# Preparing the sums of w_out for the half-block products earlier, splitting g on two engines, and four output buffers

## The chip, the cores and the metric

One core of one Trainium2 chip runs the whole program. The metric is the device time of one launch in microseconds, the median of three runs of the kernel before: 937.75 us (937.01 to 939.1). Engines are named as in the profile: PE (TensorE), DVE (VectorE), ACT (ScalarE), POOL (GpSimd) and SP (SyncE, which here issues every DMA).

## The reference, cut to what matters

Attention over 4 batches of 8 heads, 576 positions and 64 dimensions per head, with a causal mask and a decay taken from f, and behind it two feed-forward layers:

```python
x = attention(q, k, v, f)                 # 2304 tokens x 512
h = x @ w_in                              # 512 -> 2048
x = relu(h) ** 2 @ w_out                  # 2048 -> 512
h = x @ w_in2
g = where(h >= 1, h, where(h <= -1, 0, (h + 1) ** 2 / 4))
out = g @ w_out2
```

q, k, v and f are float32, the weights float64; the result is float32.

## The kernel before

**Precision.** Each float32 operand of a large product is held as a high and a low half (type fp32r), and each product is three matmuls: high by high, low by high, high by low. So every activation is split before PE uses it: one copy (the high half) and one subtraction (the low half). Weights arrive as 64-bit words, are decoded and split once during the first block, and are kept in DRAM in split form (scr0 to scr31, one for each of 16 chunks of 128 hidden units in each of two layers); all later blocks read them from there.

**Tiling.** The 2304 tokens are cut into four blocks of 512, 512, 512 and 768. The first three go through 96 steps: block, layer (mo), chunk fc of 128 hidden units. A step does 12 matmuls for h (h_group), the activation and split on ACT, DVE and POOL (act_group), and 12 matmuls that add to four output accumulators in PSUM (out_group). The attention of the next block runs between these steps: its products on PE, its softmax on DVE and ACT, and a transposition of the probabilities by DMA (PT<-PP). When a block's second layer is done, finish copies the accumulators to "o" buffers on ACT or DVE and stores them.

**The last block** (function last_block) has two halves of 384 tokens. Hidden chunks are taken in eight pairs, and each pair is a 2 by 2 block product done with seven products instead of eight (a Strassen scheme). That needs sums of the four quarters A11, A12, A21, A22 of the pair's w_out, S1 = A21 + A22, S2 = S1 - A11, S3 = A11 - A21, S4 = A12 - S2, and sums of the four quarters of g (held in G, sums t1 to t4). For each layer there are three phases. In phase A, pair by pair: h for four quarters, the activation into G, the sums of g, and three products (key a with A11, key c with S1, key b with S2). In phase B come the products with S4 and S3, in phase C those with the other quarters. The keys a, b and c are three pairs of accumulators; between the phases their contents are added up on DVE (p, u, w).

In phase A of the kernel before each pair loads its w_out chunks (wo<-scr), adds high and low half to full precision (wf), forms S1 to S4 (sf), splits them (sum), uses S1 and S2 at once and stores S3 and S4 to DRAM for phase B. All this is 10 vector operations, which the planner may put on DVE, POOL and in part ACT.

**Order.** Nothing is ordered by hand. Each operation is given to a planner (class Schedule) with a due time, its dependencies, its buffers and a cost for each engine that may run it. The planner walks through time, gives each engine the operation with the earliest due time among those that can start, repeats this with due times corrected from behind for several sets of weights, keeps the best, and emits the instructions in that order; each engine, and SP's DMA queue, runs its instructions strictly in order. A ring is a set of buffers of one shape, reused in turn; an operation that needs a buffer waits until the old user of it is done. Some rings: big (6, weights), wf (2), low (1), ghl (2), gh (3), gl (2), o (2), acc (4 PSUM banks).

Lines of the kernel before which the rows name: L1080 h and L1131 to L1133 output products of the first three blocks, L1282 h and L1226 to L1228 products of the last block, L1306 activation of the second layer in the last block, L1188 and L1190 additions on DVE and POOL, L608, L611, L613 copies on ACT, DVE and POOL, L620 and L622 subtractions on DVE and POOL, L904 the attention's product with v.

Of the kernel before, what the change touches and what calls it, by code (L numbers as in the profile page):

```python
# [8 lines left out]
F32 = mybir.dt.float32  # L9
# [345 lines left out]
def dve_t(n):  # L355
    return n / 960.0 + 0.07
# [27 lines left out]
NPAIR = NFC // 2  # L384


@with_exitstack
def tile_attention_moe_moe(ctx: ExitStack, tc: tile.TileContext, qkv, f, w2, outT):
# [56 lines left out]
    ring("sum", 2, [P, 4, 2, 256], F32R, late=True)  # L445
    ring("ghl", 2, [P, 2, HALF], F32R, late=True)
# [9 lines left out]
    ring("o", 2, [P, 512], F32)  # L456
# [714 lines left out]

    scr2 = [dram.tile([P, 2, 2, 256], F32, name=f"sum{i}") for i in range(2 * NPAIR)]

    def last_block():
# [7 lines left out]

        def load(due, src, dst, size, deps, bufs):
            return sch.op(due, {"SP": (dma_t(size), lambda: nc.sync.dma_start(out=dst(), in_=src()))}, deps, bufs)

        def add(due, out, a, b, width, deps, bufs, sub=False, psum=False):
            op = ALU.subtract if sub else ALU.add
            alts = {"DVE": (dve_t(width), lambda: v.tensor_tensor(out(), a(), b(), op=op), *([] if psum else [True]))}  # L1188
            if not psum:
                alts["POOL"] = (pool2_t(width), lambda: nc.gpsimd.tensor_tensor(out(), a(), b(), op=op))  # L1190
            return sch.op(due, alts, deps, bufs)

        for mo in range(2):
# [9 lines left out]
            def split(nm, due, gb, slot, deps):  # L1203

                if nm[0] in "5c" or nm[:2] == "aC":
                    ghl = new("ghl", f"ghl{nm}")
                    hi, lo = (lambda i=i: ghl.tile[:, i, :] for i in range(2))
                    bufs = [ghl]
                else:
                    gh, gl = bufs = new("gh", f"gh{nm}"), new("gl", f"gl{nm}")  # L1210
                    hi, lo = (lambda b=b: b.tile[:, :n] for b in bufs)
                src = lambda: gb.tile[:, slot, :]
                o1 = sch.op(due, copies(hi, src, n), deps, [gb, bufs[0]])
                o2 = sch.op(due + 0.5, subs(lo, src, lambda: hi().bitcast(F32), n), [o1], [gb, *bufs])
                return hi, lo, bufs, o2
# [19 lines left out]
            sums, s_store = [], []  # L1235
            pend = None
            for c in range(NPAIR):
                tA = T0 + c * t_a
                nm = f"{mo}_{c}"
                W0, W1 = new("big", f"wi{nm}"), new("big", f"wo{nm}")  # L1240
                o_w0, o_w1 = [], []
# [4 lines left out]
                for j in range(2):  # L1246
# [245 lines left out]
```

## Time and profile before

| | |
|---|---|
| three timed runs | 937.75 us median, 937.01 to 939.1 |
| the profiled execution | 942.0 us, of which the span of instructions is 940.2 us |
| PE busy | 922.1 us, 98% of the span |
| DVE, ACT, POOL busy | 705.3, 661.7, 239.0 us |
| DMA | 246.35 MB, its main queue busy 79.4% of 16 engines' span |
| granted PE clock | 1.0 of full speed throughout |

The stages in the span: attention of the first block alone up to about 45 us, the first block to about 225 us, second and third block from there to about 685 us, and the last block from about 680 us to the end, with its second layer from about 805 us. PE's idle time is 18 us in all, so the table of stretches and the list of waits are read for where these 18 us lie.

### The profile page before, as it was taken

How to read it: one execution, taken by the hardware profiler on the slowest of the kernel's cores; microseconds unless marked ns; L12 is line 12 of the kernel's file. 1: busy time of each engine (PE TensorE's matmuls, PEld its weight loads, DVE VectorE, ACT ScalarE, POOL GpSimd, SP SyncE). 2: the span in 40 equal slices, each digit the busy share in tenths (PEclk: the TensorE clock that was granted, in tenths of full speed). 3: DMA queues.
4: the chain of work that ended last, by engine and by line, in shares of the span. 5: the costliest groups of instructions: out<-in, count | busy, mean ns of one | idle time of the engine just before them, and what ended most of it. 6: DMA issues, size and time to landing. Idle time of an engine off the chain costs nothing.

```text
span 940.2 us, 14542 instructions
## 1 busy us (share of the span) xinstructions
PE 922.1 (98%) x4674; PEld 795.8 (85%) x4674; DVE 705.3 (75%) x1539; ACT 661.7 (70%) x1308; POOL 239.0 (25%) x392
## 2 busy tenths in 40 slices
PE   7999999999999999999999999999989999999998
PEld 6677778877888888888888888888889999999998
DVE  8899999899867668767777668866576656887653
ACT  7988889998878768877776777776455554455542
POOL 4300101324221322341223224242100013222234
PEclk9999999999999999999999999999999999999999
DMA  7799998997999897887789887896696656766561
GB/s 219 230 373 365 331 397 306 372 347 263 336 304 285 251 252 253 281 254 210 263 236 310 243 266 216 245 284 192 187 307 239 245 206 230 263 221 226 204 202 68
DMA packets 131868, 246.35 MB, mean 262 GB/s; under 512 B 90448, under 2 KB 91632, under 8 KB 117008
## 3 DMA queue, kind: packets, MB, share of 16 engines
q1 hardware_dynamic: 131792, 245.43, 79.4%
q8 instruction: 37, 0.61, 0.3%
q14 instruction: 39, 0.32, 0.1%
HBM read 177.57 MB, written 46.84 MB: 239 GB/s over the span
## 4 chain that ended last, share of the span: by engine, by line
PE 82%; DVE 7%; DMA 6%; ACT 3%; issue 1%; POOL 0%; ACTq 0%; DVEq 0%; POOLq 0%
PE h L1080 24%; PE h L1282 11%; PE acc L1131 8%; PE acc L1133 8%; PE acc L1132 8%; PE av L904 4%; DMA PT<-PP 2%; DMA out_dram<-o 2%; DMA wo<-scr 2%; PE s L825 2%; PE s L826 2%; PE b L1226 2%; PE b L1228 2%; PE b L1227 2%; PE a L1228 1%
## 5 line engine op out<-in xcount | busy, mean ns | idle before, releaser
L1080 PE MATMUL h<-x,whl 128*128 128x512 f32 x1128 | 291.3, 397 | 0.3 <-DVE whl L1057 0.3
L1080 PEld LDWEIGHTS h<-x,whl 128*128 128x128 f32 x1128 | 204.5, 188 | 41.6 <-issue 3.0
L1131 PE MATMUL acc<-gh,whl 128*128 128x512 f32 x384 | 152.9, 398 | 0.9 <-ACT o L608 0.9
L1133 PE MATMUL acc<-gl,whl 128*128 128x512 f32 x384 | 150.8, 393 | 0.0
L1132 PE MATMUL acc<-gh,whl 128*128 128x512 f32 x384 | 150.4, 392 | 0.0
L1133 PEld LDWEIGHTS acc<-gl,whl 128*128 128x128 f32 x384 | 72.1, 188 | 15.8
L1131 PEld LDWEIGHTS acc<-gh,whl 128*128 128x128 f32 x384 | 72.1, 188 | 14.2 <-ACT o L608 1.6
L879 DVE SCALAR_TENSOR_TENSOR PP<-E,st,PP 128x512 f16<-128x512 f32 (+2 forms) x128 | 76.6, 632 | 9.6 <-ACT PP L875 8.3
L627 DVE CUSTOM_DVE_ANT_0 E<-s,mask 128x288 f32<-128x288 f32 (+2 forms) x128 | 61.9, 500 | 28.5 <-PE s L826 16.6
L1132 PEld LDWEIGHTS acc<-gh,whl 128*128 128x128 f32 x384 | 72.2, 188 | 11.1
L842 ACT ACTIVATE E<-E,st 64x320 f32<-64x320 f32 (+2 forms) x96 | 63.6, 663 | 25.2 <-DVE st L627 15.1
L620 DVE TENSOR_TENSOR gl<-g,gh 128x512 fp32r<-128x512 f32 x76 | 55.7, 732 | 26.7 <-PE acc L1133 13.4
L1282 PE MATMUL h<-x_last,wi 128*128 128x384 f32 x384 | 72.5, 337 | 2.1 <-DVE G L1306 2.0
L1282 PE MATMUL h<-x,wi 128*128 128x384 f32 x384 | 72.5, 334 | 0.0
L875 ACT ACTIVATE PP<-E,st 128x512 f16<-128x512 f32 (+2 forms) x128 | 68.4, 591 | 5.7 <-DVE st L849 4.5
L1282 PEld LDWEIGHTS h<-x_last,wi 128*128 128x128 f32 x384 | 66.7, 188 | 4.5 <-DVE G L1306 4.4
L1282 PEld LDWEIGHTS h<-x,wi 128*128 128x128 f32 x384 | 67.1, 188 | 0.3
L613 POOL TENSOR_SCALAR pr<-PT 128x640 fp32r<-128x640 f16 (+2 forms) x55 | 32.2, 586 | 131.5 <-PE av L904 69.9
L904 PEld LDWEIGHTS av<-pr,vt 128*128 128x128 f32 x288 | 53.3, 188 | 12.9 <-ACT pr L608 1.5
L904 PE MATMUL av<-pr,vt 128*128 128x320 f32 (+2 forms) x288 | 62.1, 287 | 1.6 <-ACT pr L608 1.1
L622 POOL TENSOR_TENSOR gl<-g,gh 128x512 fp32r<-128x512 f32 x20 | 30.6, 1528 | 111.7 <-PE acc L1133 29.1
L608 ACT ACTIVATE pr<-PT 128x640 fp32r<-128x640 f16 (+2 forms) x60 | 36.1, 610 | 16.6 <-DMA PT<-PP 10.0
(352 smaller groups left out, 1904.3 us busy)
## 6 DMA issues: line engine op xcount, KB each, us to landing
whl<-scr SPq DMA_DIRECT2D x56, 1024.0 KB
raw<-in_w_dram SPq DMA_DIRECT2D x28, 1024.0 KB
scr<-whl SPq DMA_DIRECT2D x28, 1024.0 KB
wo<-scr SPq DMA_DIRECT2D x48, 512.0 KB
in<-in_qkv_dram SPq DMA_DIRECT2D x32, 608.0 KB
wi<-scr SPq DMA_DIRECT2D x32, 512.0 KB
whl<-scr SPq DMA_DIRECT2D x16, 512.0 KB
sum<-sum SPq DMA_DIRECT2D x16, 512.0 KB
```

What stands on the lines that cost most here:

```text
L608: alts["ACT"] = (act_t(n, psum), lambda: nc.scalar.activation(out(), in_(), AF.Copy))
L620: alts["DVE"] = (dve_t(n), lambda: nc.vector.tensor_sub(out(), a(), b()), True)
L627: return nc.vector.tensor_tensor_reduce(out=out, in0=ps, in1=mask[:m, OFF - q0:OFF - q0 + n], scale=scale, scalar=3e38, op0=ALU.add, op1=A ...
L842: nc.scalar.activation(Ec.tile[:m, :e], Ec.tile[:m, :e], AF.Exp, scale=-1.0, bias=nmx(), accum_out=st.tile[:m, 1, ci:ci + 1])))}, [*tops, ...
L875: nc.scalar.activation(hi, x, AF.Copy, scale=r())
L879: nc.vector.scalar_tensor_tensor(lo, x, r(), hi, op0=ALU.mult, op1=ALU.subtract)
L904: nc.tensor.matmul(av.tile[:, c0:W], vt.tile[:, kc, :, :], pr.tile[:, i, :n], start=(kc == 0 and i == 0), stop=(kc == NK - 1))
L1080: nc.tensor.matmul(ps.tile[:, :n], w.tile[:, 0, wi, kc * P:(kc + 1) * P], src.tile[:, kc, xi, :n], start=(kc == 0 and i == 0), stop=(kc == ...
L1131: nc.tensor.matmul(a.tile[:, :n], wh, gh.tile[:, :n], start=(fc == 0), stop=False)
L1132: nc.tensor.matmul(a.tile[:, :n], wl, gh.tile[:, :n], start=False, stop=False)
L1133: nc.tensor.matmul(a.tile[:, :n], wh, gl.tile[:, :n], start=False, stop=(fc == NFC - 1))
L1282: nc.tensor.matmul(ps.tile[:, :n], W0.tile[:, j, wi, kc * P:(kc + 1) * P], src.tile[:, kc, xi, k * n:(k + 1) * n], start=(kc == 0 and i == ...
```

## The change

The sums of w_out are no longer formed in the last block's phase A but by a function of their own, weight_sums, called 16 times (8 pairs, two layers) from the loop over steps, at steps spread over the second and third block. Each call loads the two w_out chunks of a pair from DRAM into the wf ring, forms the four sums, splits them into the same wf buffers and stores both to a DRAM tensor of twice the size (scr2). Phase A then loads only A11 in split form (256 KB) and the split S1 and S2 (512 KB); phase B loads S3 and S4 as before.

Along with that: the split of g (function split) uses ACT and DVE for the copy and DVE alone for the subtraction; before, POOL could do both. The sums of g are no longer offered to POOL. The ring sum goes, ghl has four buffers instead of two, o has four instead of two. Two products of phase C (key a, pairs 0 and 1: EARLY = 2) are moved ahead of phase B. Some due times change: the first product of a pair, its split and the first sum of g are due earlier.

```diff
+EARLY = 2
+SUM_AT = [2 * NFC + (4 * NFC - 4) * i // (2 * NPAIR) for i in range(2 * NPAIR)]
...
-    ring("sum", 2, [P, 4, 2, 256], F32R, late=True)
-    ring("ghl", 2, [P, 2, HALF], F32R, late=True)
+    ring("ghl", 4, [P, 2, HALF], F32R, late=True)
...
-    ring("o", 2, [P, 512], F32)
+    ring("o", 4, [P, 512], F32)
...
+    scr2 = [dram.tile([P, 2, 2, 512], F32, name=f"sum{i}") for i in range(2 * NPAIR)]
+    sum_op = {}
+
+    def weight_sums(i, due):
+        mo, c = divmod(i, NPAIR)
+        W = [new("wf", f"ws{nm}_{j}") for j in range(2)]
+        Sf = new("low", f"sf{nm}", [P, 4, 256], F32)
+        for j, Wj in enumerate(W):
+            o_w = load(due - 8, ..., P * 4096, [scr_op[pr, 1]], [Wj])
+            o_f.append(add(due, full, full, rest, 512, [o_w], [Wj], slack=2.0))
+        o1 = add(due + 2, S[0], A21, A22, 256, o_f, [*W, Sf])
+        o3 = add(due + 2, S[2], A11, A21, 256, o_f, [W[0], Sf], sub=True)
+        o2 = add(due + 3, S[1], S[0], A11, 256, [o1], [W[0], Sf], sub=True)
+        o4 = add(due + 4, S[3], A12, S[1], 256, [o2], [W[1], Sf], sub=True)
+        for q in range(2):
+            o = sch.op(due + 5, copies(hi, src, 512), [o1, o2, o3, o4], [Sf, W[q]])
+            o = sch.op(due + 6, subs(lo, src, ..., 512), [o], [Sf, W[q]], 0.5)
+            sum_op[i].append(load(due + 12, lambda q=q: W[q].tile, lambda q=q: scr2[i][:, q],
+                                  P * 4096, [o], [W[q]], 2.0))
...
-                o1 = sch.op(due, copies(hi, src, n), deps, [gb, bufs[0]])
-                o2 = sch.op(due + 0.5, subs(lo, src, lambda: hi().bitcast(F32), n), [o1], [gb, *bufs])
+                o1 = sch.op(due, copies(hi, src, n, "ACT DVE"), deps, [gb, bufs[0]])
+                o2 = sch.op(due + 0.5, subs(lo, src, lambda: hi().bitcast(F32), n, "DVE"), [o1], [gb, *bufs])
...
+            for c in range(EARLY):
+                o_l = load(tB - 9, lambda pr=pr: scr[pr][:, 1, :, :256], ..., P * 2048, [scr_op[pr, 1]], [wb])
+                sp = split(f"aB{mo}_{c}", tB - 4, G[c], 2, [g_op[c]["b21"]], True)
+                product(tB - 2.5 + c * t_p, "a", wb, ..., [o_l], sp, False, False, True)
...
             w_load(s + LAG)
+            for i in range(2 * NPAIR):
+                if s == SUM_AT[i]:
+                    weight_sums(i, V[s] + 3)
```

Because the planner sees other operations, it orders everything anew, from the first microseconds on. Three places are shown.

SP's DMA queue in the second block, before. Names: whl are weight chunks of a step, in a head's q, k and v, K and Q rows for the decay, PT the transposed probabilities.

```order
L985 DMA whl34_2590<-scr2_148 128x2048
L1062 DMA scr31_177<-whl29_2421 128x1024
L886 DMA_TRANSPOSE PT0_0_2640<-PP0_0_0_2625 128x6x64
L886 DMA_TRANSPOSE PT0_0_2640<-PP0_0_1_2630 128x8x128
L985 DMA whl35_2669<-scr3_149 128x2048
L886 DMA_TRANSPOSE PT0_0_2640<-PP0_0_2_2636 128x9x128
```

The same place with the change. ws0_0 are the two buffers of the first sum.

```order
L1174 DMA ws0_0_0_2577<-scr0_146 128x1024
L986 DMA whl34_2589<-scr2_148 128x2048
L1063 DMA scr31_177<-whl29_2425 128x1024
L1174 DMA ws0_0_1_2621<-scr1_147 128x1024
L887 DMA_TRANSPOSE PT0_0_2637<-PP0_0_0_2616 128x6x64
L887 DMA_TRANSPOSE PT0_0_2637<-PP0_0_1_2623 128x8x128
L887 DMA_TRANSPOSE PT0_0_2637<-PP0_0_2_2644 128x9x128
```

The two loads of the first sum stand ahead of the transposes of the first head.

PE at the start of the last block, before. acc2_1 are the third block's accumulators, a0, b0, c0 those of the last block's first layer; all share four PSUM banks.

```order
L1228 MATMUL b0_0_7750<-gl6_0_0_7720,sum0_0_7616 128x384
L1282 MATMUL h0_1_10_7757<-x3_5138,wi0_1_7493 128x384 x3
L1226 MATMUL c0_0_7765<-ghl5_0_0_7681,sum0_0_7616 128x384
L1227 MATMUL c0_0_7765<-ghl5_0_0_7681,sum0_0_7616 128x384
L1228 MATMUL c0_0_7765<-ghl5_0_0_7681,sum0_0_7616 128x384
L1226 MATMUL c0_1_7773<-ghl5_0_0_7681,sum0_0_7616 128x384
```

The same place with the change.

```order
L1257 MATMUL a0_1_7896<-ghl1_0_0_7825,wo0_0_7637 128x384
L1132 MATMUL acc2_1_3_6710<-gh95_7734,whl95_7540 128x512
L1133 MATMUL acc2_1_3_6710<-gh95_7734,whl95_7540 128x512
L1134 MATMUL acc2_1_3_6710<-gl95_7745,whl95_7540 128x512
L1291 MATMUL h0_1_00_7908<-x3_5327,wi0_1_7681 128x384 x12
L1255 MATMUL c0_0_7932<-ghl5_0_0_7864,wo0_0_7637 128x384
```

The products a0 now come ahead of the last accumulation of the third block, and 12 matmuls of h stand between that and the first product c0.

DVE in phase A of the last block's second layer, before: one pair.

```order
L620 TENSOR_TENSOR sum1_3_9229<-sf1_3_9149,sum1_3_9229 128x2x256 x2
L1188 TENSOR_TENSOR wf1_4_9247<-wo1_4_9192 128x512
L1306 SCALAR_TENSOR_TENSOR G1_2_9218<-r1_2_11_9240,h1_2_11_9195 128x384
L1188 TENSOR_TENSOR sf1_4_9267<-wf1_4_9247 128x256
L1306 SCALAR_TENSOR_TENSOR G1_2_9218<-r1_2_00_9258,h1_2_00_9236 128x384
L1188 TENSOR_TENSOR sf1_4_9267<-wf1_4_9247 128x256
L620 TENSOR_TENSOR gl1_1_2_9289<-G1_2_9218,gh1_1_2_9278 128x384
```

The same pair with the change.

```order
L1178 TENSOR_TENSOR G1_1_9173<-G1_1_9173 128x384
L1315 SCALAR_TENSOR_TENSOR G1_2_9292<-r1_2_11_9320,h1_2_11_9276 128x384
L1315 SCALAR_TENSOR_TENSOR G1_2_9292<-r1_2_00_9337,h1_2_00_9316 128x384
L621 TENSOR_TENSOR ghl1_1_2_9350<-G1_2_9292,ghl1_1_2_9350 128x384
L1178 TENSOR_TENSOR G1_2_9292<-G1_2_9292 128x384
L1315 SCALAR_TENSOR_TENSOR G1_2_9292<-r1_2_10_9358,h1_2_10_9333 128x384
```

The operations on sum, wf and sf are gone from between the activations of G. Over the whole program the sums' 160 vector operations stand on DVE 119 times, on ACT 13 and on POOL 28 times; on DVE twelve of the 16 sums stand ahead of the first operation on the last block's G, and the other four within the last block's first layer.

## Rows read from the trace of the kernel before

**Rows 1.** The page: span, busy time, chain that ended last.

```profile
span 940.2 us, 14542 instructions
PE 922.1 (98%) x4674; PEld 795.8 (85%) x4674; DVE 705.3 (75%) x1539; ACT 661.7 (70%) x1308; POOL 239.0 (25%) x392
...
PE 82%; DVE 7%; DMA 6%; ACT 3%; issue 1%; POOL 0%; ACTq 0%; DVEq 0%; POOLq 0%
```

**Rows 2.** Stretches: length, busy time by engine, granted clock, DMA share, GB/s.

```profile
0.00:30.00 30.00, 24.56 (x155) 18.71 (x155) 24.96 (x102) 23.36 (x75) 12.98 (x35) 1.00 0.82 242
30.00:130.00 100.00, 99.47 (x487) 76.46 (x487) 95.34 (x180) 87.01 (x160) 11.31 (x10) 1.00 0.90 336
130.00:230.00 100.00, 99.95 (x466) 78.68 (x467) 91.65 (x162) 91.14 (x144) 26.75 (x17) 1.00 0.89 333
230.00:330.00 100.00, 98.44 (x471) 82.35 (x470) 74.08 (x182) 79.37 (x166) 26.00 (x57) 1.00 0.96 290
330.00:430.00 100.00, 100.00 (x484) 84.28 (x483) 74.82 (x181) 75.77 (x156) 31.05 (x63) 1.00 0.83 252
430.00:530.00 100.00, 99.55 (x479) 83.64 (x478) 71.27 (x177) 71.69 (x150) 26.45 (x57) 1.00 0.86 267
530.00:630.00 100.00, 99.54 (x478) 83.37 (x478) 75.02 (x181) 76.70 (x160) 33.01 (x61) 1.00 0.82 247
...
700.00:750.00 50.00, 50.00 (x290) 50.00 (x290) 35.14 (x70) 27.14 (x55) 2.48 (x4) 1.00 0.67 235
```

**Rows 3.** PE's waits over the whole span: total, times, longest.

```profile
PE c L1226 <- ACT o L608: 2.5, 1, 2.5
PE s0q L681 <- DMA QK<-setup: 2.3, 1, 2.3
PE h L1282 <- DVE G L1306: 2.0, 4, 1.1
PE warm L580 <- POOL tiny L516: 1.4, 1, 1.4
PE av L904 <- ACT pr L608: 1.1, 1, 1.1
PE acc L1131 <- ACT o L608: 0.9, 2, 0.5
...
PE c L1226 <- DVE w L1188: 0.7, 2, 0.5
...
PE a L1228 <- DVE gl L620: 0.3, 1, 0.3
```

**Rows 4.** The chain of waits, in order: start, length, what.

```profile
272.32 10.00 DMA PT<-PP
...
684.02 7.38 DMA out_dram<-o
```

**Rows 5.** ACT's timeline at the last block's start.

```profile
691.51 1.23 ACT L608 ACTIVATE o<-acc 128x512 f32<-128x512 f32 x2 [5.68 <-DMA out_dram<-o]
```

**Rows 6.** DVE's timeline in the last block's second layer.

```profile
870.18 1.29 DVE L620 TENSOR_TENSOR sum<-sf,sum 128x512 fp32r<-128x512 f32 x2 [1.41 <-POOL sum L613]
871.40 1.78 DVE L1188 TENSOR_TENSOR wf<-wo 128x512 f32<-128x512 f32 x1
```

**Rows 7.** POOL's timeline there.

```profile
871.09 1.54 POOL L1190 TENSOR_TENSOR wf<-wo 128x512 f32<-128x512 f32 x1 [0.94 <-DMA wo<-scr]
```

**Rows 8.** Groups by line, whole span (DVE): count, busy, mean ns.

```profile
L620 DVE TENSOR_TENSOR sum<-sf,sum 128x512 fp32r<-128x512 f32 x32 | 21.3, 700 | 14.7 <-POOL sum L613 14.7
L1188 DVE TENSOR_TENSOR wf<-wo 128x512 f32<-128x512 f32 x26 | 18.8, 730 | 10.4 <-DMA wo<-scr 9.9
L1188 DVE TENSOR_TENSOR sf<-wf 128x256 f32<-128x256 f32 x29 | 13.2, 454 | 3.1 <-POOL wf L1190 2.7
```

**Rows 9.** DMA's main queue from 225 to 300 us: packets, MB, share.

```profile
q1 hardware_dynamic: 16894, 22.47, 98.4%
```

**Rows 10.** The same queue from 100 to 200 us.

```profile
q1 hardware_dynamic: 5666, 34.74, 92.8%
```

More of the change, by code (lines that the diff above doesn't have):

```diff
@@ L1170, in attend, with load, add @@
                 attention(t)
-    scr2 = [dram.tile([P, 2, 2, 256], F32, name=f"sum{i}") for i in range(2 * NPAIR)]
+    def load(due, src, dst, size, deps, bufs, slack=0.0):
+        return sch.op(due, {"SP": (dma_t(size), lambda: nc.sync.dma_start(out=dst(), in_=src()))}, deps, bufs, slack)
+    def add(due, out, a, b, width, deps, bufs, sub=False, psum=False, slack=0.0, pool=True):
+        op = ALU.subtract if sub else ALU.add
+        alts = {"DVE": (dve_t(width), lambda: nc.vector.tensor_tensor(out(), a(), b(), op=op), *([] if psum else [True]))}
+        if pool and not psum:
+            alts["POOL"] = (pool2_t(width), lambda: nc.gpsimd.tensor_tensor(out(), a(), b(), op=op))
+        return sch.op(due, alts, deps, bufs, slack)
@@ L1181, in last_block @@
         x2_ops = {}
[L1183 to L1191, printed above, removed]
         for mo in range(2):
@@ L1233, in product @@
                 return [last[key, i] for i in range(2)]
-            sums, s_store = [], []
-            pend = None
             for c in range(NPAIR):
@@ L1245, in last_block @@
                                      P * 4096, [scr_op[pr, 0]], [W0]))
-                for j in range(2):
-                    pr = mo * NFC + 2 * c + j
-                    o_w1.append(load(tA - 6, lambda pr=pr: scr[pr][:, 1], lambda W1=W1, j=j: W1.tile[:, j].bitcast(F32),
-                                     P * 4096, [scr_op[pr, 1]], [W1]))
-                Wf, Sf, Sb = new("wf", f"wf{nm}"), new("low", f"sf{nm}", [P, 4, 256], F32), new("sum", f"sum{nm}")
-                o_f = [add(tA + 2, lambda Wf=Wf, j=j: Wf.tile[:, j], lambda W1=W1, j=j: W1.tile[:, j, 0].bitcast(F32),
-                           lambda W1=W1, j=j: W1.tile[:, j, 1].bitcast(F32), 512, [o_w1[j]], [W1, Wf]) for j in range(2)]
@@ L1324, in last_block @@
+                e5 = product(te + t_p, "c", W1, lambda W1=W1: W1.tile[:, 0, 0, 0], lambda W1=W1: W1.tile[:, 0, 1, 0],
+                             [o_sb], sp5, first, stop)
+                e6 = product(te + 2 * t_p, "b", W1, lambda W1=W1: W1.tile[:, 0, 0, 1], lambda W1=W1: W1.tile[:, 0, 1, 1],
+                             [o_sb], sp6, first, stop)
             tB = T0 + NPAIR * t_a + 2
@@ L1389, in last_block @@
                     for z, key, slot, dep, e in ((0, "a", 2, "b21", 0), (256, "b", 0, "t4", 1)):
+                        if key == "a" and c < EARLY:
+                            continue
                         t1 = t0 + (2 * j + e) * t_p
```

79 lines of the change are left out of this document (41 added, 38 removed).

## The prediction

> **What bounds the kernel now.** Read the page first: PE is busy 922.1 us of a span of 940.2, and 82% of the chain that ended last is PE [rows 1]. The granted clock is 1.00, the higher of its two levels (2.4 GHz), in every stretch [rows 2], so the clock has nothing to give. The number of matmuls is the same with the change (a product that is moved is still done once), so what can be won is only PE's idle time, 18.1 us, and what can be lost is new idle time. The second thing to read is therefore the stretches [rows 2], and the third who made PE wait [rows 3]. PE idles 5.4 us in the first 30 us, then almost not at all: 0.53 and 0.05 us in the two stretches up to 230 us, 1.56 from 230 to 330, 0.00, 0.45 and 0.46 in the next three, 0.00 from 700 to 750. By name, the waits in reach of the change are 2.5 us of a product c for ACT's copy to o, 0.9 us of the accumulations L1131 for the same kind of copy, 2.0 us of h for DVE's G and 0.3 us of a for DVE's gl in the last block's second layer, and 0.7 us of c for the additions w between two phases [rows 3]. That is 6.4 us, 0.7% of the time: no more than about that can be gained.
>
> **Four o buffers.** PE's longest wait is at the last block's start: ACT could not copy the third accumulator because both o buffers were still being stored; it sat idle 5.68 us [rows 5], and the store behind that took 7.38 us in the DMA queue [rows 4]. With four buffers no copy of a block's end waits for a store. I take 3.2 of the 3.4 us (2.5 + 0.9): the copies themselves remain, 1.23 us for two [rows 5], and in the new order PE has 12 matmuls of h before the first product c, 12 x 172 ns = 2.1 us (50.00 us for 290, rows 2), to cover them. Below, the gain is 1.5 us, if the products a that now come first in line wait for the first two copies.
>
> **Two products moved ahead of phase B.** They are 12 matmuls, 2.1 us of PE work, while DVE forms w and u. The wait there was 0.7 us in two places [rows 3], so I take all 0.7; below 0, if their own split comes late.
>
> **Sums out of the second layer's phase A.** There the sums stand between the activations of G on DVE: at 870.18 us DVE waits 1.41 us for POOL's copy of a sum, and then the addition wf takes 1.78 us [rows 6] against a mean of 0.730 [rows 8], because POOL's addition of the same kind runs from 871.09 to 872.63 [rows 7]. The Trainium skill (SBUF — State Buffer, SBUF: two separate sides) has this as a lock: a DVE instruction with two SBUF inputs and a GpSimd instruction that reads SBUF exclude each other for a whole instruction. The trace agrees: 1.78 is the 1.23 us to POOL's end and 0.55 more. By that rule the 28 vector operations of the sums that stay on POOL can each hold DVE up once wherever they stand, which is one ground for the second rival below. With all sums gone from this layer and g split without POOL, I take 1.8 of the 2.3 us; the chain h, ACT twice, DVE is as long as before and may keep the rest, so the gain lies between 0 and 2.3. G's split on ACT and DVE alone is costed at nothing: 21.3 + 18.8 + 13.2 = 53 us of sums leave DVE in the last block [rows 8] but for a quarter of them, and cover what DVE takes over from POOL; without that cover, the 1.8 us are not won (third rival).
>
> **The sums in their new place.** Each is two adds of 512 columns, four of 256, two copies and two subtractions, 2 x 0.730 + 4 x 0.454 + 2 x 0.700 us = 4.7 us and the copies [rows 8] if all is on DVE, and 4 transfers of 0.52 MB. Twelve of 16 stand in the second and third block. On DVE that is at most 12 x 4.7 = 56 us in some 440, 13% over the 74% of rows 2: 87%, less than the 95% and 92% of the first block, where PE lost 0.53 and 0.05 us per 100. So DVE's load alone is no reason to stall. What the rows do not show is a sum's wait in front of an operation that feeds PE. Bounds: 0 per sum, since in the first layer of the last block PE waits for nothing from 700 to 750 us while the sums are formed; 2.3 us for the second layer's eight sums, 0.29 each, or 4.6 us for 16. A gain from the sums' new place itself is excluded: nothing that PE waits for in these blocks becomes earlier by them.
>
> DMA is nearer to its end. Between 225 and 300 us its queue is busy 98.4% [rows 9], and there PE has its only wait for the attention, 1.1 us for a copy of PT [rows 3], which came 10.00 us after its transposition was issued [rows 4]. From then on PE ran from 330 to 430 us without a gap [rows 2]: a wait shifts PE back against the queue, so it does not return at once. With the sums the queue is about as full through both blocks. I take two more such waits, 2.2 us, and 0.1 us for each of the four sums in the last block's first layer, 2.6 us together; it lies between the bounds of 0 and 4.6, and the DMA event is the nearest row.
>
> **The start.** The planner orders the first microseconds anew. Of 5.4 us idle before 30 us and 0.53 after [rows 2], 2.3 and 1.4 are for the first load and the first constant [rows 3] and stay; 2.2 us are left that may vanish or double. I take 0, bounds -2.2 and +2.2.
>
> **The sum.** -3.2 - 0.7 - 1.8 + 2.6 + 0 = -3.1 us, against the profiled execution: 942.0 (its span of 940.2 and 1.8 around it) becomes 938.9. The runs shown have a median of 937.75, 4.25 below the profiled one; the same difference on it gives 934.6 us.
>
> **The rivals.**
>
> *Sums in front of PE's work.* Twelve sums between the operations of 64 steps, on three engines that all run in order, and 28 of their operations on POOL. For it: what the sums did in the second layer. Against it: the first layer's eight sums and the first block at 95% of DVE without a wait. All 16 sums at 0.29 us cost 4.6, and the two DMA waits 2.2 more make 6.8 at worst; with 4.6 to 6 the sum is -1.1 to +0.3, some 937.2 us: no change.
>
> *A full DMA queue: slower.* Place: second and third block, where weights, q, k, v and transposes share one queue. Twelve sums add 48 x 0.524 = 25.2 MB. At the rate of a queue that is busy with large transfers, 34.74 MB in 92.8 us [rows 10] = 374 GB/s, that is 67 us. The four stretches from 230 to 630 leave 4 + 17 + 14 + 18 us free in 400 [rows 2], 58 in 440. It decides from the point at which the demand is over the room; then PE waits for weights, 67 - 58 = 9 us, and the sum is -5.7 + 0.4 + 9 = +3.7: 941.4 us. For it: these numbers as they stand, and the 98.4%. Against it: the share counts the time that packets took, overlapping ones perhaps more than once, the 374 GB/s are themselves a mean over small and large transfers, and sums may slide back since nothing in these blocks needs them. The Trainium skill (DMA: Bandwidth & Descriptors, Specifications) gives a core about 358 GB/s from HBM; by bytes alone at that figure, 264 GB/s before and 57 more would leave room and this rival would not exist. But rows 9 show the queue full at some 300 GB/s, so the busy share decides and not the bytes.
>
> *The last block's waits stay.* The waits for G could come from the chain of activation itself. For it: they are named G and gl and not a sum; against it: rows 6. Then 1.8 us are not won: -1.3, 936.4 us.
>
> **How the numbers follow.** Forecast 0.55, with a range of its own from 931.5 to 936.8; sums in front of PE's work 0.20; full queue 0.17; waits that stay 0.08. Two runs of this kernel can be told apart by about 0.2%, 1.9 us. Faster than that, below 935.9: 0.53 of the forecast, 0.07 of the first and the third rival, 0.60. Slower, above 939.6: 0.15 of the full queue and 0.03 of the first rival, 0.18. The rest, 0.22, is no change. All gains (6.4), no cost and a good start would be 929; the range begins at 931.0, which leaves out some 0.04, and ends at 939.9, which leaves out most of the full queue, 0.15.
>
> **What would show it.** Right: no wait of PE for ACT's o at any block's end; the stretch from the second layer's start to the last phase without waits for G; PE over 99.3% busy between 230 and 680 us; the DMA share there at 0.95 or more, with one to three waits of the attention's products for PT. Wrong: PE waiting for weights (whl) in the second and third block, several waits per 100 us there, or a start with over 7.5 us idle up to 30 us.

## The result and the profile after

The changed kernel takes 951.1 us (948.04 to 951.45) against 937.98 us of the kernel before (937.01 to 939.1) on the same chip: ratio 1.0132, 95% interval 1.0108 to 1.0156. It is slower by 13.1 us, where 3.1 us less were forecast. On a second chip, with more runs, the same two kernels gave 948.92 and 939.75 us, 1.0089 (1.007 to 1.0108). So the loss is 8 to 13 us.

The profiled execution of after took 950.8 us. First the page: span, busy time, and the chain that ended last, to set beside [rows 1].

```profile
span 949.0 us, 14607 instructions
...
PE 923.2 (97%) x4674; PEld 797.5 (84%) x4674; DVE 748.5 (79%) x1642; ACT 634.7 (67%) x1271; POOL 193.2 (20%) x326
...
PE 69%; DVE 12%; DMA 11%; ACT 3%; issue 2%; POOL 1%; SPq 0%; DVEq 0%; ACTq 0%; POOLq 0%
```

PE has the same 4674 matmuls and is busy 1.1 us longer; the rest of the longer span is idle time. The chain has passed from PE (82% before) to DMA (6% to 11%) and DVE (7% to 12%). The stretches of after, in the columns of [rows 2], say where:

```profile
0.00:30.00 30.00, 24.05 (x154) 19.01 (x156) 23.77 (x100) 23.16 (x73) 13.67 (x34) 1.00 0.81 231
30.00:130.00 100.00, 98.68 (x483) 76.94 (x480) 97.58 (x181) 86.55 (x165) 10.18 (x8) 1.00 0.93 336
130.00:230.00 100.00, 98.33 (x459) 76.50 (x458) 96.62 (x160) 88.10 (x141) 13.34 (x15) 1.00 0.91 334
230.00:330.00 100.00, 96.18 (x459) 80.00 (x457) 79.65 (x193) 73.03 (x154) 24.40 (x48) 1.00 1.07 321
330.00:430.00 100.00, 95.37 (x451) 78.70 (x452) 80.34 (x193) 70.23 (x148) 37.48 (x64) 1.00 1.01 284
430.00:530.00 100.00, 99.79 (x481) 83.65 (x480) 81.44 (x199) 70.99 (x152) 37.44 (x67) 1.00 1.03 316
530.00:630.00 100.00, 98.93 (x476) 82.78 (x475) 85.13 (x197) 73.05 (x155) 36.53 (x65) 1.00 1.00 296
630.00:680.00 50.00, 46.60 (x217) 38.80 (x216) 37.86 (x91) 31.96 (x67) 16.90 (x25) 0.97 1.02 281
680.00:700.00 20.00, 20.00 (x104) 18.11 (x103) 10.67 (x22) 8.81 (x17) 1.32 (x3) 1.00 0.78 247
700.00:800.00 100.00, 99.94 (x573) 99.13 (x572) 60.90 (x123) 46.37 (x92) 0.85 (x1) 1.00 0.83 278
800.00:900.00 100.00, 100.00 (x577) 99.55 (x576) 58.53 (x113) 50.11 (x95) 1.11 (x1) 1.00 0.52 175
```

The table below takes the length of each stretch less PE's busy time, for both kernels (those of before by the same view; its stretches from 630 us on, busy 50.00, 17.45, 99.80, 97.50 and 34.51 of 35 us up to 935, are not among the rows shown ahead).

| PE idle, us | before | after | difference |
|---|---|---|---|
| 0 to 30 | 5.4 | 5.9 | +0.5 |
| 30 to 230, first block | 0.6 | 3.0 | +2.4 |
| 230 to 680, second and third block | 2.5 | 13.1 | +10.7 |
| 680 to 935, last block | 5.7 | 0.1 | -5.6 |

Together +8.0, and 1.1 us of longer matmuls: 9.1 against 8.8 us between the two spans. The other 4.3 us of the 13.1 stand at no place in the profile of after: the profiled execution of before (942.0 us) lay 4.0 us above the median of 937.98, that of after 0.3 below its own.

So the last block gave about what was forecast, and more than that was lost in front of it. From 680 us on no wait of PE is listed for after at all; ACT's 5.68 us in front of a copy to o [rows 5] and the operations of sums between the activations of the second layer [rows 6, 7] have nothing that answers to them. From 230 to 680 us PE's waits are these (what PE waited with, for whom, total, times, longest):

```profile
PE h L1081 <- DVE mm L628: 3.4, 1, 3.4
PE s L826 <- DVE xs L923: 3.0, 1, 3.0
PE h L1081 <- DVE x L1150: 1.9, 3, 1.0
PE av L905 <- DVE st L628: 1.6, 1, 1.6
PE h L1081 <- DVE st L628: 1.0, 1, 1.0
PE s L826 <- DVE carry L923: 0.8, 1, 0.8
PE av L905 <- DVE pr L612: 0.5, 1, 0.5
```

They name operations of the attention (st, mm: softmax statistics; pr: the copy of PT; xs and carry: its end) and, for 1.9 us, the split of a layer's output (x), never a weight (whl) and never a sum. Behind the longest of them stands DMA. The chain of after through the 3.4 us wait, in order of time (start, length, what):

```profile
649.44 9.85 DMA PT<-PP
...
659.41 0.49 DVE pr L612
659.91 0.36 DVE E L628
660.27 0.02 DVE mm L628
...
660.34 3.87 PE h L1081 x9
```

The transposed probabilities came 9.85 us after their issue began; DVE, which runs in order, stood at pr with the statistics mm behind it, and PE stood at h. The other long links of this chain from 230 to 680 us are of the same sort: eight more pieces of DMA of 6.5 to 9.0 us (in, PT, ws). One late transposition stood in before too [rows 4]; what has changed is how often and how long DVE waits for one from 230 to 680 us (total, times, longest), in before and in after:

```profile
DVE pr L611 <- DMA PT<-PP: 8.2, 7, 2.6
```

```profile
DVE pr L612 <- DMA PT<-PP: 17.5, 13, 5.3
```

And the main queue there, packets, MB, share of 16 engines, first of before:

```profile
q1 hardware_dynamic: 102456, 114.69, 84.4%
```

and of after:

```profile
q1 hardware_dynamic: 107307, 135.31, 102.3%
```

In the 75 us of [rows 9], the queue of after reads:

```profile
q1 hardware_dynamic: 14139, 24.17, 104.5%
```

From 230 to 680 us it is 20.6 MB more, and a queue that was free 15.6% of 450 us, or 70 us, is full. The 17.9% that the share rose by are 81 us, more than the 55 us that 20.6 MB take at the 374 GB/s that I had put on them [rows 10]. The first run below shows how the 81 us divide.

### The profile page after: what moved, and what is told of

It is laid out like the page before. It is cut to its first block, busy times and chain, and to the rows that moved or that the text cites. A ratio compares the mean times of both kernels' runs of the same rounds, so it can differ in the third digit from the quotient of the medians.

```text
span 949.0 us, 14607 instructions
## 1 busy us (share of the span) xinstructions
PE 923.2 (97%) x4674; PEld 797.5 (84%) x4674; DVE 748.5 (79%) x1642; ACT 634.7 (67%) x1271; POOL 193.2 (20%) x326
## 4 chain that ended last, share of the span: by engine, by line
PE 69%; DVE 12%; DMA 11%; ACT 3%; issue 2%; POOL 1%; SPq 0%; DVEq 0%; ACTq 0%; POOLq 0%
PE h L1081 18%; PE h L1291 14%; PE acc L1132 6%; PE acc L1134 6%; PE acc L1133 6%; DMA in<-in_qkv_dram 5%; DMA PT<-PP 5%; PE av L905 2%; PE b L1255 2%; PE b L1257 2%; PE b L1256 2%; DVE PP L880 1%; PE c L1255 1%; PE c L1257 1%; PE s L826 1%
## 5 line engine op out<-in xcount | busy, mean ns | idle before, releaser
L1081 PEld LDWEIGHTS h<-x,whl 128*128 128x128 f32 x1128 | 206.7, 189 | 53.7 <-DVE mm L628 3.7
L880 DVE SCALAR_TENSOR_TENSOR PP<-E,st,PP 128x512 f16<-128x512 f32 (+2 forms) x128 | 79.1, 647 | 8.1 <-ACT PP L876 7.7
L876 ACT ACTIVATE PP<-E,st 128x512 f16<-128x512 f32 (+2 forms) x128 | 69.8, 591 | 14.2 <-DMA PT<-PP 6.8
L628 DVE CUSTOM_DVE_ANT_0 E<-s,mask 128x288 f32<-128x288 f32 (+2 forms) x128 | 62.6, 499 | 20.6 <-PE s L827 19.6
L843 ACT ACTIVATE E<-E,st 128x576 f32<-128x576 f32 (+2 forms) x96 | 63.4, 661 | 21.7 <-DVE st L840 11.6
L614 POOL TENSOR_SCALAR pr<-PT 128x640 fp32r<-128x640 f16 (+2 forms) x60 | 39.0, 652 | 116.1 <-PE av L905 64.3
L623 POOL TENSOR_TENSOR gl<-g,gh 128x512 fp32r<-128x512 f32 x19 | 26.5, 1396 | 135.1 <-PE acc L1134 50.9
L1178 DVE TENSOR_TENSOR G<-G 128x384 f32<-128x384 f32 x64 | 34.9, 555 | 20.4 <-ACT G L1307 19.8
```

What stands on the lines that cost most here:

```text
L614: alts["POOL"] = (pool_t(n), lambda: nc.gpsimd.tensor_scalar(out(), in_(), 1.0, 0.0, op0=ALU.mult, op1=ALU.add))
L628: return nc.vector.tensor_tensor_reduce(out=out, in0=ps, in1=mask[:m, OFF - q0:OFF - q0 + n], scale=scale, scalar=3e38, op0=ALU.add, op1=A ...
L843: nc.scalar.activation(Ec.tile[:m, :e], Ec.tile[:m, :e], AF.Exp, scale=-1.0, bias=nmx(), accum_out=st.tile[:m, 1, ci:ci + 1])))}, [*tops, ...
L876: nc.scalar.activation(hi, x, AF.Copy, scale=r())
L880: nc.vector.scalar_tensor_tensor(lo, x, r(), hi, op0=ALU.mult, op1=ALU.subtract)
L1081: nc.tensor.matmul(ps.tile[:, :n], w.tile[:, 0, wi, kc * P:(kc + 1) * P], src.tile[:, kc, xi, :n], start=(kc == 0 and i == 0), stop=(kc == ...
```

## The experiments

The theories. **Q**: the transfers of the sums fill the DMA queue of the second and third block, and the attention's loads and transpositions come late. **V**: the 160 vector operations stand in front of what feeds PE on engines that run in order. Later there were two more. **P** is the plan: the planner's choice of weighting, and its price of a transposition. The price is 0.75 us on the mean by its formula; the queue at [rows 9] leaves some 1.45 us for each of 15, an estimate from 73.8 us busy less 19.5 MB of other transfers at the 374 GB/s of [rows 10]. **H**: SP stands in order at a sum's load, with the transpositions behind it. "Idle" is PE's idle time from 230 to 680 us in the profile; before has 2.5, after 13.1.

### Data or vector work

**Order of after, sums without data.**

```diff
-            o_w = load(due - 8, ..., lambda pr=pr: scr[pr][:, 1], lambda Wj=Wj: Wj.tile, ...)
+            o_w = load(due - 8, ..., lambda pr=pr: scr[pr][:4, 1], lambda Wj=Wj: Wj.tile[:4], ...)
...
-            sum_op[i].append(load(due + 12, lambda q=q: W[q].tile, lambda q=q: scr2[i][:, q],
+            sum_op[i].append(load(due + 12, lambda q=q: W[q].tile[:4], lambda q=q: scr2[i][:4, q],
```

> The changed kernel in the same order on every engine, but the 64 transfers of the sums move 4 partitions instead of 128 (16 KB instead of 512 KB each), their first additions read a constant, and the last block reads w_out where it read sums. Left out: the values of the sums. All 160 vector operations stay. Theory Q (the DMA queue is over its capacity in the second and third block, and what arrives late there holds PE up): PE's idle time from 230 to 680 us falls from 13.1 us to 4 or less, DMA share there to about 0.86, total about 941 us. Rival V (the sums' vector operations stand in front of what feeds PE): idle time and total stay, 949 to 951 us.

Measured: 936.98 us, 0.9967 (0.9953 to 0.998) of before; idle 2.5. The queue from 230 to 680 us:

```profile
q1 hardware_dynamic: 103125, 115.01, 90.4%
```

DVE's wait for the transpositions is below that of before again:

```profile
DVE pr L617 <- DMA PT<-PP: 5.3, 6, 2.2
```

All vector work of the sums and all of after's order are there, and the loss is gone; what is left is a gain of 0.3%. The time came lower than Q expected, since the whole 10.7 us went, and the share higher (0.90, expected 0.86).

This run also divides the 81 us, by the shares. With 0.3 MB more than before the share is 6.0% higher: 27 us come with after's order and its small transfers, without the bytes, and what makes them up is not shown. The other 11.9%, 54 us, are the 20.3 MB that after moves beyond this run: 379 GB/s, about the 374 of [rows 10]. Neither part alone fills the 70 us that were free; both together do.

**Order and transfers of after, no vector work.**

```diff
+        if idle:
+            alts = quiet(alts)          # same cost to the planner, nothing emitted
...
-            ... 512, [o_w], [Wj], slack=2.0))
+            ... 512, [o_w], [Wj], slack=2.0, idle=True))
```

> The changed kernel in the same order, all 64 transfers of the sums at full size, but none of their 160 vector operations (left out: the sums themselves; what is stored is w_out as it was loaded). Theory Q: the total stays within 2 us of the changed kernel, 949 to 951 us, and the idle time from 230 to 680 us at 11 us or more. Rival V: it falls by 9 or 10 us, to about 941 us.

Measured: 950.13 us, 1.0104 (1.0075 to 1.0133); idle 11.9. The queue:

```profile
q1 hardware_dynamic: 108430, 135.84, 101.7%
```

DVE was busy 70% to 76% there, as before the change, and PE lost nearly as much as after. V fell.

**Order of before, 48 copies of 512 KB from DRAM to DRAM in the second and third block.**

```diff
+                    if s >= 2 * NFC and s % 4 != 3 and last:
+                        nc.sync.dma_start(out=waste[s], in_=scr[s % 32][:, 1])
```

> The kernel before, in its own order, with 48 transfers added that nothing waits for: 512 KB each from DRAM to DRAM, behind three of four weight loads in the second and third block. No vector operation is added and no buffer is used. Theory Q: PE's idle time from 230 to 680 us rises from 2.5 us to 9 to 14, total 945 to 950 us. Rival V, or a third theory, that the planner's new order alone costs the time: 938 to 939 us.

Measured: 958.92 us, 1.0199 (1.0171 to 1.0227): more than expected. Idle 12.8, and 2.3 us between 700 and 800; PE's matmuls also took 6.8 us longer (928.9 against 922.1 us busy), with a granted clock of 0.98 in three stretches of 100 us. The queue, and the first of PE's waits:

```profile
q1 hardware_dynamic: 108589, 137.02, 100.2%
```

```profile
PE av L904 <- ACT pr L608: 5.4, 3, 2.8
PE av L904 <- ACT r L1112: 2.5, 1, 2.5
```

Bytes that nobody uses and no sum waits for do harm of the same kind in before's own order, and PE waits again at the attention. With the two runs above, Q is shown from both sides.

### The output buffers, and SP's waits

**After with two output buffers.**

```diff
-    ring("o", 4, [P, 512], F32)
+    ring("o", 2, [P, 512], F32)
```

> The kernel after with two output buffers in place of four, nothing else. My prediction put 3.2 us on the four buffers. If that is right, the waits of PE for outputs' stores in the last block come back (2 to 3 us there) and the time is 953 to 955 us. If the last block's waits went for other reasons (the products formed early, the sums out of the way), it is 950 to 952 us, no different from the kernel after. Q and V say nothing on it.

Measured: 951.06 us, 1.0103 (1.0072 to 1.0134), no different from after. ACT again stood 6.5 us for a store before a copy to o at the last block's start, but PE's only wait from 680 us on was

```profile
PE c L1255 <- ACT o L609: 0.7, 1, 0.7
```

At the second block's start it waited once more, where after has no such wait:

```profile
PE acc L1132 <- ACT o L609: 0.8, 1, 0.8
```

So in this plan two buffers bring back 1.5 us of the 3.4 (2.5 and 0.9) of [rows 3]. That is all that the four buffers can account for; the rest went with the new order, which at the last block's start puts 12 matmuls of h and the products a in between. Which of the two does it there was not tried.

**After with a third wf buffer** (H, first try).

```diff
-    ring("wf", 2, [P, 2, 512], F32)
-    ring("o", 4, [P, 512], F32)
+    ring("wf", 3, [P, 2, 512], F32)
+    ring("o", 2, [P, 512], F32)
```

> The kernel after with two output buffers (as in the run that was no different from after, 1.0103 of before), the room given to a third buffer of the ring wf, in which the sums' loads, results and stores live, and the weighting 0.6 of the kernel after. All transfers stay. If the queue's load takes the time (Q), SP's 21.7 us of waits for sums' stores fall to under 8 us, but the queue stays over 97% of 230 to 680 us, PE's waits there at 8 us or more, and the time at 1.008 to 1.014 of before. If the wait at the head of SP's queue is what holds the transpositions back, PE's waits fall under 4 us and the time to 1.003 of before or less.

(The edit also fixes the weighting at 0.6, the one that after has.) Measured: 959.43 us, 1.0201 (1.0168 to 1.0234); idle 15.1. The condition did not come about: in the planner's new order SP's waits for the stores of sums grew to 29.1 us. It says nothing on H.

**Order of after, the stores' bytes moved by copies that nobody waits for** (H, second try).

```diff
+                nc.sync.dma_start(out=scr2[i][:4, q], in_=W[q].tile[:4])
+                nc.sync.dma_start(out=waste[2 * i + q], in_=scr[mo * NFC + 2 * c + q][:, 1])
```

> The kernel after with the 32 stores of sums cut to 4 of 128 partitions, and behind each a copy of 512 KB from DRAM to DRAM that nothing waits for, so that the queue carries the same bytes; the last block reads w_out in the place of the sums. Every engine's order is that of after. SP's 21.7 us of waits of sums' loads for sums' stores should fall to 5 to 10 us. If the full queue takes the time (Q), the queue's share of 230 to 680 us stays about 1.00, PE's waits there at 8 to 14 us, and the time at 1.009 to 1.015 of before. If the waits at the head of SP's queue do, PE's waits fall to 2 to 5 us, as with no data, and the time to 0.997 to 1.003 of before.

SP's wait at the loads of sums (L1174), in after:

```profile
SPq L1174 <- DMA sum<-ws: 21.7, 10, 5.3
```

and here:

```profile
SPq L1174 <- DMA sum<-ws: 2.5, 3, 1.3
```

Idle stayed at 11.9 us, the queue's share at 101.4%; 948.51 us, 1.0072 (1.005 to 1.0094). As that ratio is under the first one of after, both kernels ran once more on one chip.

> The kernel after, unchanged, as the partner of the next run on the same chip. 1.010 to 1.015 of before if chips do not differ; 1.006 to 1.009 if this chip is milder to it.

> The kernel with the cut stores and the copies that nothing waits for, once more (the last block reads w_out in the place of the sums). If the full queue takes all of the loss, it is within 0.2% of the kernel after on the same chip. If SP's waits for the stores of sums take half of it, it is 0.4% to 0.8% below it.

Measured: after 948.92 us, 1.0089 (1.007 to 1.0108); with free stores 946.96 us, 1.0091 (1.0065 to 1.0118). The ratios differ by 0.02%, where half of the loss would be 0.45%: H fell as the cause, and the full queue is what is left. A small part of H stays open: the two medians lie 2.0 us apart, and idle is 10.6 us in after and 8.5 us with free stores. The two chips differ by more than this edit does.

### The plan: weighting

The planner makes a plan for each of ten weightings of DVE and POOL and keeps one for the whole program: DVE 0.8 for before, 0.6 for after. In the first block no sum stands, but there the additions of decode left POOL. POOL's row of before, 30 to 230 us (after has none):

```profile
L1022 POOL TENSOR_TENSOR wf<-wf,low 128x1024 int32<-128x1024 int32 x8 | 19.5, 2440 | 63.0 <-DVE wf L1018 48.2 <-ACT wf L1001 11.8 <-ACT low L1010 3.1
```

DVE's row for the same additions, of before (22) and of after (30):

```profile
L1021 DVE CUSTOM_DVE_ANT_0 wf<-wf,low 128x2048 uint16<-128x2048 uint16 x22 | 27.7, 1260 | 0.8
```

```profile
L1022 DVE CUSTOM_DVE_ANT_0 wf<-wf,low 128x2048 uint16<-128x2048 uint16 x30 | 39.8, 1327 | 0.8
```

**Before with after's weighting, after with before's.**

```diff
-WEIGHTS = [{}, *({"DVE": x, "POOL": x * y} for x in (0.4, 0.6, 0.8) for y in (0.0, 0.5, 1.0))]
+WEIGHTS = [{"DVE": 0.6, "POOL": 0.0}]      # and 0.8 for the kernel after
```

> The kernel before, planned with DVE's weighting 0.6 alone, as the planner kept it for after, in place of 0.8. No sums, transfers or buffers are moved by hand. If the weighting is the first block's loss, PE waits 2.5 to 3 us between 30 and 230 us (before: 0.6) and the time is 940 to 943 us. If the first block's loss comes from something else of the change (the pools in SBUF, the four output buffers), the first block is as in before and the time within 1.5 us of it.

> The kernel after, planned with DVE's weighting 0.8 alone, as the planner kept it for before, in place of 0.6. All transfers and sums are those of after. If the weighting is the first block's loss, POOL has 5 to 9 additions of decode between 30 and 230 us, PE waits 0.6 to 1.0 us there (after: 3.0) and 2 us are won. If the queue takes the time of the second and third block whatever the plan is (Q), PE's waits of 230 to 680 us stay at 8 to 15 us and the time is 945 to 952 us. If they came from after's plan, they fall under 4 us and the time is 936 to 940 us.

Measured: before with 0.6: 947.44 us, 1.0068 (1.0043 to 1.0093). Its first block, with no sum in the program's second and third block:

```profile
30.00:130.00 100.00, 98.64 (x482) 76.94 (x479) 97.54 (x179) 86.53 (x163) 10.19 (x8) 1.00 0.93 338
130.00:230.00 100.00, 98.30 (x451) 76.84 (x450) 95.82 (x159) 87.28 (x140) 13.94 (x17) 0.98 0.91 332
```

After with 0.8: 952.97 us, 1.0142 (1.0106 to 1.0178). Its first block, and its worst stretch:

```profile
30.00:130.00 100.00, 99.73 (x489) 77.30 (x487) 94.73 (x183) 88.35 (x158) 13.06 (x12) 1.00 0.94 339
130.00:230.00 100.00, 99.53 (x469) 77.94 (x466) 92.43 (x159) 91.53 (x153) 18.12 (x15) 1.00 0.90 339
...
430.00:530.00 100.00, 93.03 (x432) 76.30 (x431) 74.82 (x177) 69.48 (x144) 32.42 (x59) 0.98 1.04 300
```

The first block's 2.4 us go with the weighting, in both directions. The second and third block's do not: idle is 14.2 us with 0.8 too, 2.9 in before with 0.6. After's loss is the same size under another plan, at a queue share of 99.9%. Before with 0.6 lost 6.1 us, more than its 940 to 943 us expected. Its span is 6.3 us longer: 4.1 us of idle time, and 2.2 us of longer matmuls (924.3 against 922.1 us busy), with a granted clock of 0.98 from 130 to 230 us and 0.96 from 680 to 700.

### The plan: the price of a transposition, and less traffic

Eight kernels, from three edits. (a) is the price in the planner, from 0.75 to 1.63 us on the mean (one expectation below puts it at 1.45):

```diff
-            ... {"SP": ((0.625, 0.1125 * blocks * m / P, 1.23, 1.2), transpose)}, ...
+            ... {"SP": ((0.625, 0.245 * blocks * m / P, 1.23, 1.2), transpose)}, ...
```

(b) moves the second layer's eight sums into the last block's first layer (and SUM_AT has eight entries):

```diff
+                if mo == 0:
+                    weight_sums(NPAIR + c, tA + 4)
```

(c) reads w_out from the steps' own weight buffers, so that a sum needs no loads, and calls for one sum at every fourth step:

```diff
-            o_w = load(due - 8, lambda pr=pr: scr[pr][:, 1], ...)
+            hb, ops = whl[u + j], whl_op[u + j]
+            his, los = (lambda hb=hb, z=z: hb.tile[:, 1, z].bitcast(F32) for z in range(2))
```

Before with (a):

> The kernel before with only the planner's price of a transposition raised to 0.245 us per block; no work is added or moved by hand. Theory Q: the queue has room (share 0.84), so 935 to 941 us, within 3 us of before. If the raised price leads to bad orders by itself, 945 us or more.

After with (a):

> The changed kernel, only the planner's price of a transposition in the queue is raised from 0.1125 to 0.245 us per block of 128 rows, 0.75 to 1.63 us on the mean, which is about what the trace of before shows between 225 and 300 us (98.4% busy, 19.5 MB of plain transfers at 374 GB/s, 15 transpositions: 1.45 us each). The planner then spreads the sums out by itself: 9 and not 12 of them are loaded before the last block. Theory Q with the planner's price as its cause: idle time from 230 to 680 us falls to 5 to 7 us, total 942 to 945 us. If the queue is too full in any order: 948 us or more.

After with (b):

> The changed kernel with only the first layer's eight sums in the second and third block, the second layer's eight while the last block's first layer runs. Loads and stores as in the change. In the two blocks 17 MB are added instead of 25, a share of 0.95. Theory Q: idle time from 230 to 680 us 4 to 8 us, total 939 to 945 us, the last block still without waits. If the last block's first layer has no room for eight sums, PE idles 2 us or more there.

After with (a) and (b):

> The kernel after with the second layer's eight sums in the last block's first layer (so 16 of the 32 loads and 16 of the 32 stores, 16.8 MB, leave the second and third block) and the planner's price of a transposition raised from 0.75 to 1.45 us mean. Without the price this split gave 942.9 us with 5.3 us of PE's waits between 230 and 680 us. If those waits come from the planner counting on room in the queue that transpositions fill (Q with the wrong price), they fall to about 1 us and the time to 937 to 939 us. If the queue is simply too full at a share of 1.00 whatever the order is (Q alone), 941 to 944 us. If the higher price makes one collapse like that at 460 to 495 us of the kernel with all sums in the two blocks, 948 us or more.

After with (c), then with (a) and (c):

> The changed kernel, but the sums take w_out from the weight buffers of the steps that PE is using anyway, so the 32 loads of the sums fall away and 32 stores stay; one sum every four steps, eight in each of the two blocks. The vector work is that of the changed kernel. The queue has 16.8 MB more than before instead of 25 in those blocks, at 374 GB/s 45 us in 450, so a share of about 0.94 against 0.84 before and 1.02 changed. Theory Q: PE's idle time from 230 to 680 us 4 to 7 us, total 937 to 943 us. If vector work or the order counts, 948 us or more as in the changed kernel.

> The same with the planner's price of a transposition raised to 0.245 us per block. If the price is what made the planner count on room in the queue that is not there: idle time from 230 to 680 us 3 us or less, total 933 to 938 us. If the raised price itself leads to a bad order (one collapse of PE at the third block's start cost the earlier run with that price some 14 us and the clock), such a collapse is seen here too, total 945 us or more.

After with all three, and the same with the weighting 0.8:

> As the split with the true price, but the first layer's eight sums read w_out from the buffers in which their steps hold it, so the second and third block get 16 stores (8.4 MB) and no loads for them. Q with the wrong price: this has the least traffic of all kernels with sums there, so PE's waits of 230 to 680 us are under 1 us and the time is 935 to 938 us, of which the last block's 5.5 us are the gain and the first block's 2.4 us the loss. If reading the steps' own buffers is what costs (DVE late for a buffer's next load), it stays at 941 us or above, as the kernel with all sums read so.

> The fastest kernel so far with the change (first layer's eight sums read from the steps' buffers in the second and third block, second layer's in the last block, the true price of a transposition; 0.9979 of before) planned with DVE's weighting 0.8 alone in place of 0.6. If the first block's 2.4 us are the weighting's, they come back and the time is 936 to 937.5 us, 0.995 to 0.997 of before. If the order that goes with 0.8 brings the second and third block other waits, or one collapse at the third block's start, it is 939 us or more.

| kernel | us | of before | queue 230 to 680 | idle |
|---|---|---|---|---|
| before, (a) | 939.32 | 0.9988 (0.997 to 1.0006) | 88.3% | 0.0 |
| after, (a) | 970.45 | 1.0316 (1.0272 to 1.0359) | 100.1% | 14.3 |
| after, (b) | 942.91 | 1.0022 (1.0002 to 1.0043) | 100.2% | 5.3 |
| after, (a) (b) | 963.69 | 1.0246 (1.0218 to 1.0274) | 96.3% | 17.4 |
| after, (c) | 959.93 | 1.0218 (1.0172 to 1.0263) | 95.7% | 21.0 |
| after, (a) (c) | 941.37 | 1.0009 (0.9999 to 1.0019) | 98.3% | 5.9 |
| after, (a) (b) (c) | 938.68 | 0.9979 (0.9964 to 0.9995) | 96.9% | 1.6 |
| the same, weighting 0.8 | 946.86 | 1.0069 (1.0052 to 1.0086) | 97.8% | 3.8 |

What follows: half of the sums moved out, (b), brings back most of the loss, as Q would have it, though the share stays at 100.2%. But the price does not do what I expected of it. It takes 18.6 us off the kernel with (c) and puts some 20 us on the two without (c), and the kernel with (c) alone idles most at the lowest share of the seven kernels with the change in this table. So once the queue is over some 95%, the plan decides as much as the bytes, and the share alone does not tell the idle time. For (c) alone the traces show one wait more: DVE and POOL stood 12.8 and 10.6 us for stores of sums in front of additions that write the same buffers, and 0.8 and 0.2 us with the price. That this makes the difference was not tried.

In the kernels with the price and without (c), nearly all idle time is one collapse at the third block's start. After with (a), in stretches of 5 us:

```profile
455.00:460.00 5.00, 5.00 (x24) 4.14 (x23) 4.07 (x13) 4.06 (x8) 0.00 (x0) 1.00 1.04 351
460.00:465.00 5.00, 2.09 (x12) 1.58 (x11) 3.28 (x5) 4.80 (x12) 2.13 (x6) 1.00 1.03 424
465.00:470.00 5.00, 2.80 (x8) 2.01 (x9) 3.79 (x10) 1.00 (x3) 0.14 (x1) 0.63 1.10 375
...
480.00:485.00 5.00, 2.43 (x8) 1.63 (x8) 4.72 (x11) 2.63 (x7) 3.25 (x6) 0.50 0.70 180
485.00:490.00 5.00, 1.72 (x9) 1.61 (x7) 3.91 (x11) 4.34 (x11) 1.53 (x3) 0.50 0.42 80
...
495.00:500.00 5.00, 5.00 (x26) 4.22 (x25) 3.34 (x8) 4.10 (x9) 0.00 (x0) 1.00 0.99 300
```

The chain of waits from 460.00 to 490.98 us in this trace has no piece of DMA: ACT and DVE hand the attention's operations (E, PP, pr, xs) to one another, and PE stands for each. So this collapse does not look like the late transfers of after. The clock adds to it: PE's matmuls take 9.6 us longer than before's over the whole span (931.7 against 922.1 us). In front of the collapse SP issued four stores of the block's output in 3.38 us from 458.59 us on, and the next transposition's issue took 4.38 us. That these four stores start it was not tried, and the cause stays open. The last kernel, with 0.8, was a miss of another kind: its first block is whole again (0.7 us idle), but the last block's first layer lost 7.4 us, 4.1 of them for its weights (wi), with the loads and stores of the second layer's sums now in that stretch.

The kernel with all three edits is the fastest of those with the change that compute everything: 938.68 us against 940.47, 0.2% under before. Its first block still carries the weighting 0.6.

## Why the prediction was wrong, point by point

**What bounds the kernel.** Right: PE's matmuls stayed, and all that moved is its idle time. "No more than 6.4 us can be gained" held; the order of after without the sums' data is 3 us faster than before.

**The last block, -3.2, -0.7 and -1.8.** Right in sum: 5.7 us forecast, of which up to 0.9 lay at the starts of the second and third block [rows 3]; 5.6 found in the last block alone. The waits for o, for w and u, for G and gl are all gone. That the numbers agree so closely is in part luck, since one cause was half wrong: the -3.2 were put on four buffers, and with two only 1.5 us of waits come back and the time is the same within the noise. The rest is the new order, of which the step named the 12 matmuls of h.

**The sums in their new place, +2.6: the step that failed.** Its vector half was right: DVE stayed under the 87% bound (79.65 to 85.13% busy in the four stretches), and without the vector work the loss stays. Its DMA half failed, "I take two more such waits, 2.2 us", with 4.6 us as the upper bound of the step; it measured 10.7 us. I took the one wait that the trace had [rows 3, 4] as the measure of a queue that was not yet full, and so counted events where I had to set demand against room. [rows 9] had shown the point at which it turns: 98.4% with before's traffic alone.

**A full DMA queue, the rival with 0.17.** This is what happened: right place, and 9 us against 10.7. Its time, 941.4 us, was still too low, as it had neither the first block's 2.4 us nor any change of the base. Its grounds against itself fell: the sums did not slide back, and shares that count overlaps (102.3% is more than full) still told when the room was gone. Its size is in part luck. The bytes' rate was about right (379 GB/s against 374), but their 55 us alone would have gone into the 70 us free from 230 to 680 us; what was in no term are the 27 us that the run without data shows beyond before. And PE never waited for whl; the attention's inputs and transpositions, which are used soon after their issue, come late first. The Trainium skill (DMA: Bandwidth & Descriptors, Specifications) gives a core about 358 GB/s from HBM. In the four stretches from 230 to 630 us the traffic was 284 to 321 GB/s with the share at 1.00 to 1.07, so the trace shows the queue full below that figure.

**Sums in front of PE's work, 0.20.** Fell with V. The lock between DVE and POOL, which was one ground for it, can have cost little of the loss: the run without vector work took POOL's operations of the sums away too, and lost nearly as much.

**The start, 0.** The first 30 us were right (+0.5). The step looked at these 30 us alone; that a plan made anew could cost 2.4 us in the 200 us behind them, by another weighting, was in no term.

**The base.** The differences of the two profiles (8.8 us) and of the two medians (13.1, and 9.2 on the other chip) are not the same; the forecast carried the profile's offset of 4.25 us from before to after as if it were fixed, and it was not.

## What to carry to other kernels

Work that is moved out of a stage takes its transfers with it: before you call a place free, set the added queue time against the queue's free share there, not against PE's or DVE's, and leave a margin: here 27 of the 70 us that were free went without any of the added bytes. When the queue is full, look for the loss at whatever needs its data soonest after issue, not at the loads that were added. And when a planner orders the whole program anew, read the stretches far from the change too: one global choice of it can cost more than the part that was edited.

## What was not expected of the hardware

The granted clock falls behind PE's idle time. In the collapse above it fell from 1.00 to 0.63 in the two stretches in which PE was busy 2.09 and 2.80 of 5 us. It was 0.69 and 1.00 in the two that are left out there, then 0.50, the lower of the two levels (1.2 GHz), for 10 us, and 1.00 again with PE busy throughout. In after the same is seen once, behind the wait for the transposition of 649.44 us:

```profile
655.00:660.00 5.00, 1.94 (x10) 1.30 (x8) 0.58 (x2) 0.83 (x2) 1.90 (x3) 1.00 1.07 187
660.00:665.00 5.00, 4.66 (x14) 3.80 (x15) 4.25 (x13) 3.38 (x8) 1.94 (x4) 0.66 1.02 418
665.00:670.00 5.00, 5.00 (x27) 4.34 (x26) 3.86 (x13) 3.50 (x10) 0.62 (x1) 1.00 0.69 130
```

Nine matmuls of h took 3.87 us from 660.34 us on, in the chain above. Nine of the same shape, 10 us later in the same trace:

```profile
670.46 2.13 PE h L1081 x9
```

So the wait of 3.4 us cost some 1.7 us more in a clock that was not granted. A stretch can look busy and still be slow; the granted clock has to be read beside the busy time.
